# Moving 32x32 turns behind masks on VectorE, and divides ahead of squares on GpSimd, in a fused threshold attention and squared-ReLU MLP

## The chip, the cores and the metric

One core of one Trainium2 chip runs the whole kernel. The metric is the device time of one execution in microseconds; lower is better. All times quoted are medians.

In the profile lines PE is TensorE, PEld its loading of weights, DVE is VectorE, ACT is ScalarE, POOL is GpSimd, and SPq is the queue in which SyncE issues DMAs. L303 is line 303 of the kernel, and `out<-in` names the tiles that an instruction writes and reads. A DMA "lands" when its data are in place.

## The reference

```python
# q, k, v: (8 batches, 8 heads, 576, 64) fp32
scores = q @ k^T / 8                       # (576, 576) per head
thresh = max(scores, -1) - 0.02
scores = where(scores >= thresh, scores, -1e9) - max
attn   = exp(scores) / (sum(exp(scores)) + 1e-9)
x      = (attn @ v) -> (4608, 512)         # heads side by side
out    = relu(x @ w_in)**2 @ w_out         # 512 -> 2048 -> 512
```

## The kernel before

A visit is one pair of heads (the four pairs of the first batch take two short visits each, so 32 pairs make 36 visits). A whole visit has five steps: i = 0 to 3 are 128 queries of both heads each, i = 4 is the last 64 queries of both heads. The MLP works on chunks of 256 tokens, whose matmuls are dealt out between the steps so that TensorE always has something to do. The second product of the MLP is made from seven smaller ones (in all chunks but the first), whose inputs are sums and differences of blocks (the "sums" below). From the twelfth visit on (25 of 36 visits) the weights are turned by VectorE in 32x32 blocks and put into place by DMAs.

Scores are written to PSUM, in which this kernel has room for the scores of one step only. The scores of step s therefore wait until the mask of step s-1 has read them:

```python
def threshold(vis, i):     # VectorE: the mask, L230, and its sums
    for u in range(n):
        nc.vector.scalar_tensor_tensor(out=wu, in0=sc[u], scalar=thr[u], in1=wu,
                                       op0=ALU.is_ge, op1=ALU.mult, accum_out=sm[u])
    nc.vector.tensor_scalar(...); nc.vector.reciprocal(rcp, den)     # L232, L233
def divide(vis, i):        # GpSimd: L240, L242
    nc.gpsimd.tensor_scalar(out=w[:, u, :], in0=w[:, u, :], scalar1=z, scalar2=rcp, op0=add, op1=mult)
```

The turn goes into `turned`, which has two areas; the five steps of a visit fill three (steps 0 and 1, steps 2 and 3, step 4), so a turn can find its area still being read by DMAs. The DMAs put the blocks into `wT`, from which the mix (weights times v) reads. I call the three batches of 16 DMAs P0, P1 and P2:

```python
def turn_blocks(vis, i):   # VectorE, L303
    nc.vector.transpose(wb[:, at:at + k1 - k0, i % 2, :], w[...])
def place_blocks(vis, pair):                       # 16 issues on SyncE's queue
    for qb in range(4):
        for j in range(4):
            nc.sync.dma_start(out=wT[...], in_=wb[...])   # L316: P0, P1; L323: P2
```

The step loop, cut to what matters; `fill(quarter)` emits a quarter of the step's MLP work, with its ReLU (ScalarE), squares and sums (GpSimd, VectorE):

```python
for s in range(END + 1):
    scores(s)                              # TensorE; maximum on VectorE, L207
    # in the 25 late visits at_once is false (but for the first two steps of the first)
    if at_once: exponents(n, i)            # ScalarE: L215, L216, exp L218
    if s in mixes: mix(*mixes[s])          # in step i == 3: the visit before; reads wT
    if 0 < s <= NST and by_dma(steps[s - 1][0]):
        m, x = steps[s - 1]
        turn_blocks(m, x)                  # the step before
        if x >= 2: place_blocks(m, x - 2)  # x = 2: P0, x = 3: P1, x = 4: P2
    fill(quarter)
    if not at_once: exponents(n, i)
    threshold(n, i)
    if last and more: prep(n + 1)          # q and k transposes of the next visit, L181
    fill(quarter)
    divide(n, i)
    fill(quarter); fill(quarter)
```

P1 is thus issued in step 4, right after the turn of step 3.

## Time and profile before

| what | value | how to read it |
|---|---|---|
| time | 1439.11 us, 1432.95 to 1439.48 | median of the first three runs |
| profiled span, clock | 1436.5 us, 0.991 | the traced execution |
| a matmul 128x256 | 383 ns long, the next starts 216 ns later | they overlap, so PE 96% busy is not PE 96% used |
| VectorE's turns (L303) | 325, 168.8 us busy, 31.2 us of waits for DMAs | the waits stand in front of whatever comes behind them |
| issues of P0, P1, P2 | 1200, 0.61 us each and 0.04 to the next | SyncE, one after the other |
| after the last mix | 161.7 us of MLP alone | the same in every kernel of this study |

The prediction shows the lines on which this rests.

### The profile page before, as it was taken

Reading aid. Unit: us, or ns where it says so; the run is one execution under the profiler, and the core shown is the slowest. Engines: PE = TensorE matmul, PEld = TensorE weight load, DVE = VectorE, ACT = ScalarE, POOL = GpSimd, SP = SyncE. Lnnn points to the kernel's source line nnn. Section 1 sums busy time; section 2 is a strip of 40 time slices with the busy share of each in tenths; the row PEclk is TensorE's granted clock in tenths of the full one; section 3 lists DMA queues with packets and bytes.
Section 4 is the critical chain, followed back from the end, with each engine's and each line's share of the span. In section 5 each row is a group of like instructions: output and inputs, shape, how many; then the busy total and the mean of one; then the engine's idle time right before and its main releaser. Section 6 shows DMA issues by size and latency. Waiting matters only on the chain.

```text
span 1436.5 us, 22320 instructions
## 1 busy us (share of the span) xinstructions
PE 1381.1 (96%) x7460; PEld 1066.3 (74%) x7460; DVE 855.2 (60%) x1847; ACT 440.0 (31%) x1080; POOL 772.3 (54%) x1015
## 2 busy tenths in 40 slices
PE   5898989999999999999999999999999999999998
PEld 3676656777777778777777787777777877778887
DVE  5998886875656665656566666565656666401011
ACT  3765655323232223232222232222222222210100
POOL 2687787745554555555464665554546564422332
PEclk9998999999999999999999999999999999999999
DMA  7664441454454545554545455554454556310000
GB/s 150 130 140 111 127 114 41 79 99 89 85 104 84 107 86 113 98 112 82 96 90 101 88 107 91 111 96 92 82 96 89 107 91 112 69 26 9 7 15 15
DMA packets 507201, 127.14 MB, mean 89 GB/s; under 512 B 497488, under 2 KB 499088, under 8 KB 507088
## 3 DMA queue, kind: packets, MB, share of 16 engines
q1 hardware_dynamic: 496208, 107.78, 40.7%
q0 software_dynamic: 8496, 17.64, 4.0%
q8 instruction: 60, 0.98, 0.3%
q10 hardware_dynamic: 2384, 0.30, 0.1%
q14 instruction: 53, 0.43, 0.1%
HBM read 49.81 MB, written 9.44 MB: 41 GB/s over the span
## 4 chain that ended last, share of the span: by engine, by line
PE 59%; SPq 6%; issue 1%; DMA 1%; DVE 1%; POOL 1%; POOLq 0%; DVEq 0%
PE bank L402 24%; PE bank L468 21%; PE s L202 7%; PE bank L359 7%; SPq L316 5%; DMA wT<-turned 1%; SPq L323 1%; DVE turned L303 0%; DVE w L230 0%; POOL vs L176 0%; POOL g L413 0%; DVE gsum L486 0%; POOL vs L173 0%; DVE kT L181 0%; POOL gsum L392 0%
## 5 line engine op out<-in xcount | busy, mean ns | idle before, releaser
L402 PE MATMUL bank<-xT,w_in_sb 128*128 128x256 f32 x2304 | 522.2, 383 | 1.8 <-ACT osb L443 1.8
L402 PEld LDWEIGHTS bank<-xT,w_in_sb 128*128 128x128 f32 x2304 | 433.7, 191 | 82.1 <-issue 21.7
L207 DVE TENSOR_REDUCE st<-s 128x1 f32<-128x576 f32 x288 | 206.9, 753 | 248.2 <-PE s L202 247.8
L230 DVE SCALAR_TENSOR_TENSOR w<-s,st,w 128x576 f32<-128x576 f32 x269 | 207.4, 804 | 97.1 <-ACT w L218 96.9
L242 POOL TENSOR_SCALAR w<-w,st 128x576 f32<-128x576 f32 x269 | 237.9, 892 | 24.8 <-DVE st L233 15.2
L468 PE MATMUL bank<-wo,gsum 128*128 128x256 f32 x1088 | 249.4, 382 | 1.8 <-POOL gsum L392 1.8
L413 POOL TENSOR_TENSOR g<-g 128x512 f32<-128x512 f32 x144 | 150.1, 1045 | 156.2 <-ACT g L412 127.7
L468 PEld LDWEIGHTS bank<-wo,gsum 128*128 128x128 f32 x1088 | 204.4, 190 | 39.9 <-issue 9.8
L202 PE MATMUL s<-kT,qT 64*128 64x288 f32 x1024 | 185.7, 443 | 39.0 <-DVE w L230 19.1
L303 DVE STREAM_TRANSPOSE turned<-w 128x576 f32<-128x576 f32 (+2 forms) x325 | 168.8, 565 | 44.2 <-DMA wT<-turned 31.2
L468 PE MATMUL bank<-wo,g 128*128 128x256 f32 x816 | 188.5, 381 | 0.0
L218 ACT ACTIVATE w<-s,st 128x576 f32<-128x576 f32 x269 | 184.6, 732 | 0.4 <-ACT st L216 0.2
L202 PEld LDWEIGHTS s<-kT,qT 64*128 64x128 f32 x1024 | 105.3, 192 | 102.8 <-issue 75.0
L359 PE MATMUL bank<-wT,vs 128*64 128x128 f32 (+7 forms) x1700 | 172.5, 361 | 5.9 <-DMA wT<-turned 3.1
L468 PEld LDWEIGHTS bank<-wo,g 128*128 128x128 f32 x816 | 153.5, 190 | 28.2 <-issue 7.4
L215 ACT ACTIVATE st<-st 128x2 f32<-128x2 f32 (+1 forms) x160 | 33.4, 209 | 418.8 <-DVE st L207 418.3
L359 PEld LDWEIGHTS bank<-wT,vs 128*64 128x64 f32 (+1 forms) x1700 | 99.7, 138 | 80.2 <-issue 32.3
L240 POOL TENSOR_SCALAR st<-st 128x2 f32<-128x2 f32 (+1 forms) x160 | 39.9, 249 | 207.6 <-DVE w L230 195.0
L412 ACT ACTIVATE g<-bank 128x512 f32<-128x512 f32 x144 | 86.1, 599 | 206.5 <-PE bank L402 206.4
L482 DVE TENSOR_TENSOR gsum<-g 128x512 f32<-128x512 f32 x34 | 21.8, 676 | 110.9 <-PE bank L468 110.9
L346 ACT COPY xT<-bank 128x256 f32<-128x256 f32 x42 | 16.1, 385 | 188.5 <-PE bank L359 188.5
L185 POOL COPY qmid<-qT 64x64 f32<-64x64 f32 x64 | 18.7, 292 | 91.5 <-DVE qT L181 89.7
(68 smaller groups left out, 1009.8 us busy)
## 6 DMA issues: line engine op xcount, KB each, us to landing
wT<-turned SPq DMA_DIRECT2D x800, 72.0 KB, 2.2
ql<-in_q_dram SPq DMA_DIRECT2D x126, 72.0 KB, 2.6
out_dram<-osb POOLq DMA_DIRECT2D x34, 256.0 KB, 2.8
wo<-in_moe_w_in_dram SPq DMA_DIRECT2D x16, 512.0 KB, 4.7
wo<-in_moe_w_out_dram SPq DMA_DIRECT2D x16, 512.0 KB, 3.8
vs<-in_v_dram POOLq DMA_DIRECT2D x50, 128.0 KB, 3.5
kl<-in_k_dram SPq DMA_DIRECT2D x63, 72.0 KB, 2.4
kl<-in_k_dram SPq DMA_DIRECT2D x63, 64.0 KB, 2.5
```

What stands on the lines that cost most here:

```text
L202: nc.tensor.matmul(sc[u][:, half, 0:HALF], lhsT, kT[rows, half * HALF:(half + 1) * HALF], start=True, stop=True)
L207: nc.vector.tensor_reduce(out=mx[:, u:u + 1], in_=sc[u][:, :, 0:HALF], axis=AX.XY, op=ALU.max)
L218: nc.scalar.activation(out=w[:, u, :].rearrange("p (h k) -> p h k", h=2), in_=sc[u][:, :, 0:HALF], func=AF.Exp, bias=bias[:, u:u + 1], sca ...
L230: nc.vector.scalar_tensor_tensor(out=wu, in0=sc[u][:, :, 0:HALF], scalar=thr[:, u:u + 1], in1=wu, op0=ALU.is_ge, op1=ALU.mult, accum_out=s ...
L242: nc.gpsimd.tensor_scalar(out=w[:, u, :], in0=w[:, u, :], scalar1=z[:, u:u + 1], scalar2=rcp[:, u:u + 1], op0=ALU.add, op1=ALU.mult)
L303: nc.vector.transpose(wb[:, at:at + k1 - k0, i % 2, :], w[:, u, k0 * 32:k1 * 32].rearrange("p (k q) -> p k q", q=32))
L316: nc.sync.dma_start(out=to[:, :, at:at + 64], in_=wb[rows, j::4, :, :].rearrange("p c u q -> p c (u q)"))
L359: nc.tensor.matmul(ps[u * D:(u + 1) * D, :], vs[n % 2][rows, u * (NBLK + 1) + c, :], wT[rows, NBLK if c == NBLK else u * (NBLK + 1) + c, a ...
L402: nc.tensor.matmul(h[:, x % 2, :], w_in_sb[:, c, f * P:(f + 1) * P], xT[:, c, at:at + TCH], start=(c == 0), stop=(c == NMC - 1))
L412: nc.scalar.activation(out=to, in_=h, func=AF.Relu)
L413: nc.gpsimd.tensor_tensor(out=to, in0=to, in1=to, op=ALU.mult)
L468: nc.tensor.matmul(to, left[:, f, :], wo[:, slot, f, :], start=(f == 0), stop=(f == HF - 1))
```

## The change

The intent: the mask is what releases PSUM for the next scores, so nothing that isn't needed for it should stand before it. The turns go behind the mask, the exponents before the first quarter of MLP work, and the divide directly behind the mask instead of behind a quarter of squares.

```diff
         if on:
-            if at_once:
-                exponents(n, i)
+            exponents(n, i)
 ...
-        if 0 < s <= NST and by_dma(steps[s - 1][0]):
-            m, x = steps[s - 1]
-            turn_blocks(m, x)
-            if x >= 2:
-                place_blocks(m, x - 2)
         quarter = rate(s) / 4 if s < END else 1e9
         fill(quarter)
 ...
         if on:
-            if not at_once:
-                exponents(n, i)
             threshold(n, i)
             if last and more and not lay:
                 prep(n + 1)
 ...
+            if not at_once:
+                divide(n, i)
+        if 0 < s <= NST and by_dma(steps[s - 1][0]):
+            m, x = steps[s - 1]
+            turn_blocks(m, x)
+            if x >= 2:
+                place_blocks(m, x - 2)
         fill(quarter)
-        if on:
+        if on and at_once:
             divide(n, i)
```

## The prediction

> **What bounds the kernel now.** I read the page first, then the waits of PE and of the DMA queue of SyncE, then the timeline of single steps. A "visit" is one pair of heads: five steps i = 0 to 4, each with scores, maximum, exp, mask and divide; in 25 visits (those that this change touches) VectorE then turns each step's weights in 32x32 blocks into `turned`, and DMAs place the blocks into `wT`, in three batches of 16: P0 (steps 0 and 1), P1 (steps 2 and 3), P2 (step 4). The mix (weights times v) runs in step 3 of the following visit.
>
> The busy shares and the chain of the page:
>
> ```profile
> PE 1381.1 (96%) x7460; PEld 1066.3 (74%) x7460; DVE 855.2 (60%) x1847; ACT 440.0 (31%) x1080; POOL 772.3 (54%) x1015
> ...
> PE 59%; SPq 6%; issue 1%; DMA 1%; DVE 1%; POOL 1%; POOLq 0%; DVEq 0%
> PE bank L402 24%; PE bank L468 21%; PE s L202 7%; PE bank L359 7%; SPq L316 5%; DMA wT<-turned 1%; SPq L323 1%; DVE turned L303 0%; DVE w L230 0%; POOL vs L176 0%; POOL g L413 0%; DVE gsum L486 0%; POOL vs L173 0%; DVE kT L181 0%; POOL gsum L392 0%
> ```
>
> TensorE looks full, and VectorE and GpSimd half idle. But the chain also goes through SPq L316, a queue that only issues DMAs. The waits of that queue say what holds it:
>
> ```profile
> SPq L316 <- PE bank L359: 54.9, 24, 6.9
> SPq L316 <- DVE turned L303: 25.1, 2, 19.1
> ```
>
> 24 times, once a visit, it waits for the mix (L359) to have read `wT`; only twice for a transpose. Its timeline over one visit:
>
> ```profile
> 744.34 21.07 SPq L316 DMA_DIRECT2D wT<-turned  x32
> 765.50 11.01 SPq L323 DMA_DIRECT2D wT<-turned  x16
> 776.55 1.67 SPq L162 DMA_DIRECT2D kl<-in_k_dram  x3
> ```
>
> The mix of the visit before ended at 744.31. The 48 issues then run back to back to 776.51, the last lands at 777.77, and the next mix starts at 780.22. So the queue needs 33.5 us of the 35.9 us between the mixes: a slack of 2.45 us. Over the visits the slack runs from about 0 (417.0, 538.5) to 3.7 us and is mostly 1 to 2. The last mix of all has none: it starts at 1264.57, stops after two matmuls, and resumes at 1268.42 when P2 has landed (1268.22). **The kernel has two bounds of nearly the same length**, TensorE's program order and this loop: mix, 48 issues, landing, mix.
>
> **What TensorE itself still loses.** I took start-to-start distances: a 128x256 matmul follows the one before after 216 ns, eight score matmuls take 1.17 us. What exceeds that by over 0.15 us at a place adds up to 29.8 us between the 24 mixes of the phase 301 to 1229 us, 1.3 us a visit. A typical one:
>
> ```profile
> 406.32 1.44 DVE L303 STREAM_TRANSPOSE turned<-w 128x576 f32<-128x576 f32 x2 [1.60 <-DMA wT<-turned]
> ...
> 407.69 0.77 DVE L230 SCALAR_TENSOR_TENSOR w<-s,st,w 128x576 f32<-128x576 f32 x1
> ...
> 408.62 1.94 PE L202 MATMUL s<-kT,qT 64*128 64x288 f32 x8
> ```
>
> The turn waits 1.60 us for a DMA to free `turned`, the mask behind it is late, and the scores, which need the PSUM that the mask reads, take 1.94 us. This is what the change aims at.
>
> **What the Trainium skill says.** "PSUM — Partial Sum Buffer", section "Engine vs sequencer instructions": the queues of ScalarE, VectorE and GpSimd are strict FIFO. The mask above, stuck behind a turn, agrees, and it is what makes the order matter. "DMA: Bandwidth & Descriptors", section "Anatomy of one DMA": DMA engines do not wait on semaphores, the issuing sequencer waits before dispatch, and a DMA has a fixed cost of about 2 us. The trace agrees: the 16 issues of P1 stand in the queue until their transposes are done (254.04 us, below), and issue to landing is 2.2 us in the median. "GPSIMD Engine Reference", section "8. Key points": GpSimd shares its SBUF interfaces with VectorE, with contention when VectorE reads two SBUF inputs. It agrees: a pair of divisions takes 1.62 us, but 2.68 us at 600.68 beside the subtraction of two SBUF tiles on VectorE (600.74).
>
> **The change, part by part.** It adds and removes no arithmetic; instruction counts and TensorE's order are the same. All of it concerns the 25 late visits.
>
> 1. Exponents go ahead of the first quarter of MLP work. Where ScalarE stood behind the copies of the mix (exp 5.5 us after the maximum at 617 us), it saves the mask that time. Those steps last 11 us, so the mask wasn't late for the scores; worth about nothing by itself.
> 2. The turn goes behind the mask. The turns that wait for `turned` no longer hold up the mask: the list of waits has 31.2 us in 19 waits, most of which vanish. Upper value: the 29.8 us of stalls above.
> 3. The divide goes ahead of the squares: 269 divisions of 892 ns and their small ones start earlier, the squares (1045 ns) up to 2.0 us later. GpSimd is 54% busy. A square is late only where the sums for product 5 are due; I take 0 to 3 us in all.
> 4. **What it moves the wrong way: the turn of step 3.** Its place is step 4, on VectorE. Order now: maximum, turn of 3, mask, q and k transposes (L181) for the next visit. New order: maximum, mask, L181 twice, turn of 3. P1 can't be issued before that turn ends. One visit as it is:
>
> ```profile
> 752.42 0.76 DVE L207 TENSOR_REDUCE st<-s 128x1 f32<-128x576 f32 x1 [2.55 <-PE s L202]
> 753.10 1.55 DVE L303 STREAM_TRANSPOSE turned<-w 128x512 f32<-128x512 f32 x4
> 754.57 0.38 DVE L488 TENSOR_TENSOR osb<-bank,p1s 128x256 f32<-128x256 f32 x1
> 754.88 0.80 DVE L230 SCALAR_TENSOR_TENSOR w<-s,st,w 128x576 f32<-128x576 f32 x1
> ...
> 756.09 0.78 DVE L181 STREAM_TRANSPOSE qT<-ql 128x576 f32<-128x576 f32 x1
> 756.79 0.74 DVE L181 STREAM_TRANSPOSE kT<-kl 128x576 f32<-128x576 f32 x1
> ```
>
> The turn ends at 754.65, P0's sixteenth issue at 754.81: P1 finds its data ready by 0.16 us. In the new order exp of step 4 (about 1.1 us after the maximum) must come first, then mask, its two small operations, L181 twice, and only then 1.55 us of turn. From the mask's start to the end of L181 is 2.65 us; the mask itself can start about 0.3 us earlier. So the turn ends about 3.75 us later: 2.65 - 0.3 + 1.55 - 0.15 of overlap of neighbours on VectorE.
>
> **Sum for the loop.** The turn of 3 ends at one of two distances from the mix, by whether 24 or 32 matmuls of 216 ns lie between mix and scores of step 4: 8.6 us in 14 visits, 10.33 us in 8, 9.7 us in one. From P1's first issue to P2's landing takes 22.1 to 24.1 us, mean 23.15. New distance mix end to next mix start:
> - 14 visits: 8.6 + 3.75 + 0.1 + 23.15 = 35.6 us. Now they have 35.65 us in the mean, 34.2 to 34.3 without their stalls. Visit by visit about zero in all: stalls go, the wait for P2 takes their place.
> - 8 visits: 10.33 + 3.75 + 0.1 + 23.15 = 37.3 us against 35.8 now: +1.5 us each, +12 us.
> - The one at 9.7: +0.4 us.
> - First visit: P1 already waits for the turn (P0 issued by 265.10, turn ends 271.06, P1 starts 271.22), which shows the dependence in this trace. +3.75 less 1.4 of slack: about +2.4 us.
> - Last visit: no q and k to transpose. The turn ends some 2.3 us later, of which P0's end (1245.87 against 1244.45) hides 1.4: +0.9 us.
>
> Together 12 + 0.4 + 2.4 + 0.9 = +15.7 us. After the last mix TensorE runs MLP work alone, unchanged. 1439.1 + 15.7 = 1454.8.
>
> **Rivals.**
> - *The author's*: the mask is the late one, and the kernel gains TensorE's stalls. For it: 1.3 us a visit is really lost. Against: it needs P1 not to wait. If SyncE waited for something else, about 30 us at most would go; more likely 20, giving 1419.
> - *Transfer hidden anyway*: if the turn of 3 is later by under 2 us in the class of 8.6 (P0's issues end 10.5 to 11.5 us after the mix), those visits gain and the other eight lose a little: about 1436.
> - *GpSimd or VectorE becomes the bound*: VectorE's round is now maximum 1.42, exp 1.3 uncovered, mask and small ones 2.0, turn 1.43: 6.1 us in series, where the turn used to lie beside exp; the shortest steps are 6.5 us. With a 1.3 us subtraction between, single steps would slip, and late squares add up to 3 us. If this delays step 3 to step 4 it lies on the loop: up to 1465.
>
> **Range and chances.** The middle is 1455. Downward: a shift of 3.0 instead of 3.75 us takes about 10 us off, and one of the three runs before was 6 us under the median: 1444. Upward: extra slips between mix and the scores of step 4, each in full on the loop: 1464. Slower by 2% would be 1468, faster by 2% 1410, more than all the stalls: both unlikely.
>
> **What would show it.** Right: SyncE's L316 waits for DVE turned L303 in nearly every visit (2 before), some 2 us each; PE L359 waits for DMA wT<-turned, or starts right at the landing; eight visits stretch to about 42 us from mix to mix; DVE turned waiting for DMA (31.2 us) nearly gone; score groups of 1.87 to 1.94 us rarer. Wrong: if P1 starts right behind P0, or the turn of 3 ends under 2 us later than now, or if the time falls under 1432, the stalls were what counted. Mean matmul rows and clock (0.99) should be the same.

## The result, and the profile after

The changed kernel took 1457.14 us (four runs, 1455.09 to 1459.06) against 1439.11: 1.25% longer by the medians. The ratio is 1.0135, with a 95% interval from 1.0104 to 1.0167. A ratio here is the mean time of one kernel's fast runs over that of the other's of the same rounds, so it isn't quite the ratio of the medians. By the 2% rule the two are "same"; by the interval the change is a small loss. The predicted 1455 was 2 us off. That it came so close is partly luck: between the two traces the parts add up to 20.7 us, 5 more than the 15.7 predicted, while the medians lie only 18.0 us apart.

Busy time and the chain on the page of the changed kernel:

```profile
PE 1387.3 (95%) x7460; PEld 1071.6 (74%) x7460; DVE 880.6 (60%) x1847; ACT 440.0 (30%) x1080; POOL 762.7 (52%) x1015
...
PE 72%; SPq 11%; DVE 9%; issue 3%; DMA 2%; ACT 2%; POOL 0%; DVEq 0%; ACTq 0%; POOLq 0%
PE bank L402 27%; PE bank L468 21%; PE s L202 11%; PE bank L359 10%; SPq L323 7%; SPq L316 4%; DMA wT<-turned 2%; DVE w L230 2%; DVE st L207 2%; DVE turned L138 1%; PE bank L266 1%; PE bank L436 1%; DVE wo L426 1%; ACT w L218 1%; DVE turned L137 1%
```

The busy shares hardly differ, and would not tell that 20 us have been added. The chain does: SyncE's queue has gone from 6 to 11%. The waits (engine, line, released by, total us, times, longest) tell more:

```profile
SPq L316 <- DVE turned L303: 81.5, 26, 22.1
SPq L316 <- PE bank L359: 23.0, 21, 6.3
```

Before, the queue waited for a turn twice; now it does 26 times. And on VectorE and TensorE:

```profile
DVE turned L303 <- DMA wT<-turned: 17.1, 45, 1.8
...
PE bank L359 <- DMA wT<-turned: 14.1, 10, 3.9
```

The turns' waits for landings shrank from 31.2 to 17.1 us, as the change intended, and TensorE's waits for landings grew to 14.1 us in 10 times (3.1 us once before). The same visit as in the prediction, on VectorE (start, length, line, tiles, and in brackets the idle time before):

```profile
763.98 0.76 DVE L207 TENSOR_REDUCE st<-s 128x1 f32<-128x576 f32 x1 [2.27 <-PE s L202]
...
765.83 0.82 DVE L230 SCALAR_TENSOR_TENSOR w<-s,st,w 128x576 f32<-128x576 f32 x1 [0.76 <-ACT w L218]
...
767.76 0.74 DVE L181 STREAM_TRANSPOSE kT<-kl 128x576 f32<-128x576 f32 x1
768.42 1.52 DVE L303 STREAM_TRANSPOSE turned<-w 128x512 f32<-128x512 f32 x4
```

The maximum starts 8.1 us after the end of the mix (755.86), as before. The turn now ends 14.1 us after the mix instead of 10.3. On SyncE and TensorE:

```profile
756.15 24.48 SPq L316 DMA_DIRECT2D wT<-turned  x32
780.73 10.99 SPq L323 DMA_DIRECT2D wT<-turned  x16
```

```profile
791.59 0.75 PE L359 MATMUL bank<-wT,vs 128*64 128x320 f32 x2
793.39 4.75 PE L359 MATMUL bank<-wT,vs 128*64 128x320 f32 x38 [1.04 <-issue]
```

The 32 issues of P0 and P1 take 24.5 us instead of 21.1, since the queue stands still from 766.62 to 770.00. P2's last DMA lands at 792.98. The mix starts two of its 40 matmuls, stops, and resumes at 793.39. (The profile names no releaser for this stop, "issue"; that it is the landing is read from the 0.41 us between the two. For ten others the profile names it: the 14.1 us above.)

To say where the 20.7 us between the two traces (1436.5 and 1457.2) came from, I cut both at the ends of the mixes:

| stretch | before | after | difference | predicted |
|---|---|---|---|---|
| start to the end of the first of these mixes | 301.3 | 309.0 | +7.7 | +2.4 |
| from there to the end of the 24th | 932.9 | 944.3 | +11.4 | +12.4 |
| 24th to the last | 40.74 | 42.30 | +1.6 | +0.9 |
| after the last | 161.7 | 161.7 | 0 | 0 |

Inside the 23 mixes of the second row, stops lengthen 16 mixes by 23.8 us in all (2 mixes by 0.7 us before). So the loop added more than 11.4 us; about half of that was paid back by the waits at the scores, which fell from about 16 to about 4 us from 301 us on (what the switches to scores and back exceed their usual length by, see turn3_first).

### The profile page after: what moved, and what is told of

It reads as the page before. It is cut to its first block, busy times and chain, and to the rows that moved or that the text cites. A ratio compares the mean times of both kernels' runs of the same rounds, so it can differ in the third digit from the quotient of the medians.

```text
span 1457.2 us, 22482 instructions
## 1 busy us (share of the span) xinstructions
PE 1387.3 (95%) x7460; PEld 1071.6 (74%) x7460; DVE 880.6 (60%) x1847; ACT 440.0 (30%) x1080; POOL 762.7 (52%) x1015
## 4 chain that ended last, share of the span: by engine, by line
PE 72%; SPq 11%; DVE 9%; issue 3%; DMA 2%; ACT 2%; POOL 0%; DVEq 0%; ACTq 0%; POOLq 0%
PE bank L402 27%; PE bank L468 21%; PE s L202 11%; PE bank L359 10%; SPq L323 7%; SPq L316 4%; DMA wT<-turned 2%; DVE w L230 2%; DVE st L207 2%; DVE turned L138 1%; PE bank L266 1%; PE bank L436 1%; DVE wo L426 1%; ACT w L218 1%; DVE turned L137 1%
## 5 line engine op out<-in xcount | busy, mean ns | idle before, releaser
L402 PEld LDWEIGHTS bank<-xT,w_in_sb 128*128 128x128 f32 x2304 | 433.6, 191 | 82.4 <-issue 21.1
L242 POOL TENSOR_SCALAR w<-w,st 128x576 f32<-128x576 f32 x269 | 225.0, 844 | 24.9 <-DVE st L233 16.3
L202 PE MATMUL s<-kT,qT 64*128 64x288 f32 x1024 | 180.5, 442 | 39.7 <-DVE w L230 16.7
L359 PE MATMUL bank<-wT,vs 128*64 128x128 f32 (+7 forms) x1700 | 184.8, 362 | 19.9 <-DMA wT<-turned 14.1
L359 PEld LDWEIGHTS bank<-wT,vs 128*64 128x64 f32 (+1 forms) x1700 | 110.0, 139 | 96.1 <-issue 54.3
L303 DVE STREAM_TRANSPOSE turned<-w 128x576 f32<-128x576 f32 (+2 forms) x325 | 167.6, 563 | 18.8 <-DMA wT<-turned 17.1
L202 PEld LDWEIGHTS s<-kT,qT 64*128 64x128 f32 x1024 | 101.2, 191 | 101.8 <-issue 72.7
L143 POOL TENSOR_TENSOR turned<-turned 128x512 f32<-128x512 f32 x32 | 41.2, 1287 | 44.6 <-DVE turned L141 42.3
```

Source lines behind the costliest of these rows:

```text
L202: nc.tensor.matmul(sc[u][:, half, 0:HALF], lhsT, kT[rows, half * HALF:(half + 1) * HALF], start=True, stop=True)
L303: nc.vector.transpose(wb[:, at:at + k1 - k0, i % 2, :], w[:, u, k0 * 32:k1 * 32].rearrange("p (k q) -> p k q", q=32))
L359: nc.tensor.matmul(ps[u * D:(u + 1) * D, :], vs[n % 2][rows, u * (NBLK + 1) + c, :], wT[rows, NBLK if c == NBLK else u * (NBLK + 1) + c, a ...
L402: nc.tensor.matmul(h[:, x % 2, :], w_in_sb[:, c, f * P:(f + 1) * P], xT[:, c, at:at + TCH], start=(c == 0), stop=(c == NMC - 1))
```

## The experiments

Eleven kernels ran in three groups, each beside the kernel before on the same chip (1438.44, 1435.93 and 1436.61 us). Kernels of different groups are compared by medians, and the kernel before moved by some 3 us between the groups. The theory is that the late turn of step 3 holds P1 in the queue, and the loop of mix, 48 issues and landing becomes the bound. The rivals were that the early divides delay the squares, or that turns behind masks lengthen VectorE's round in general. The cuts by mixes of each kernel (first mix's end, to the 24th, to the last; us; without p2_from_act, which is set aside below) come first:

```
before                 301.3   932.9   40.7
after                  309.0   944.3   42.3
turn3_first            307.6   926.8   41.9
turn3_behind_alone     308.1   974.1   42.6
turn3_between          306.9   940.9   42.4
divide_late            308.6   945.6   41.5
turns_first            301.4   935.3   40.4
turn0_behind_alone     301.1   926.4   39.5
turn3_first_v0_old     301.4   926.2   40.4
turns_0_3_behind       303.4   944.5   41.6
half_p2                306.8   919.4   36.1
turn0_mask4_ahead      301.7   920.2   40.4
```

### turn3_first: one turn back

```diff
+        if 0 < s <= NST and by_dma(steps[s - 1][0]) and steps[s - 1][1] == 3:
+            ...turn_blocks, place_blocks         # ahead of fill and mask
         quarter = rate(s) / 4 if s < END else 1e9
...
-        if 0 < s <= NST and by_dma(steps[s - 1][0]):
+        if 0 < s <= NST and by_dma(steps[s - 1][0]) and steps[s - 1][1] != 3:
```

> The changed kernel, with only the turn of step 3 (and the issue of P1 behind it) put back ahead of the mask of step 4; the turns of the other four steps stay behind the masks, exponents and divide stay early. My theory (P1 held back by that turn, the loop mix - 48 issues - landing - mix is the bound): P1 again starts right behind P0, the loop needs 33.4 to 35.0 us between mixes, TensorE's own order without stalls 33.4 to 35.3, the larger of the two summed over 23 visits is 797 us against 822 in the kernel before: about 1415 to 1424 us, faster than both kernels. Rival 1 (the early divides that delay the squares cost the time) or rival 2 (any turn behind the mask lengthens VectorE's round): 1445 us or more.

Measured: 1437.26 us, ratio 0.9986 (0.9944 to 1.0028). Moving this one turn back took 20 us off the changed kernel, and P1 again starts 0.12 us behind P0 in the mean (2.11 in the changed kernel). The direction is the theory's. But the kernel isn't faster than before, and my 1415 to 1424 was a clear miss. Two causes show in the trace. First, the steady part is 6.1 us shorter than before, not 25: my figure for TensorE's stalls was too large. A switch from the MLP's matmuls to the eight score matmuls of steps 0 to 2 and back costs 0.20 us in both kernels when nothing waits: the first score starts 0.31 us after the matmul before it, and after the scores the second MLP matmul starts 0.32 us after the first, both instead of 0.216. Of the 29.8 us in the prediction about 14 are this fixed cost at 69 switches, and only about 16 us were waits. Second, the first visit still loses 6.3 us here (307.6 against 301.3), so that isn't P1's doing alone. (1.6 us more went where the granted clock fell to half for a moment, see the next run.)

### turn3_behind_alone: only the suspected part

In the kernel before, only the turn of step 3 moves behind the mask and the q and k transposes.

```diff
-        if 0 < s <= NST and by_dma(steps[s - 1][0]):
+        if 0 < s <= NST and by_dma(steps[s - 1][0]) and steps[s - 1][1] != 3:
...                                               # behind threshold and prep, ahead of fill:
+        if 0 < s <= NST and by_dma(steps[s - 1][0]) and steps[s - 1][1] == 3:
```

> The kernel before, with only the turn of step 3 moved behind the mask of step 4 and the q and k transposes; exponents, divide and the other turns as before. My theory: the full loss of the loop, about 1450 to 1457 us, with SyncE's L316 waiting for the transpose L303 in over 20 visits. Rivals 1 and 2 (divide early, or the other four turns): within 5 us of before, 1434 to 1444.

Measured: 1486.72 us, ratio 1.034 (1.0306 to 1.0375), worse than the whole change by 30 us. P1 is held back as foreseen (2.13 us behind P0), but most of the time is lost elsewhere, and the size is a miss. The waits of this kernel:

```profile
DVE turned L303 <- DMA wT<-turned: 67.9, 20, 4.9
PE s L202 <- DVE w L230: 46.1, 33, 3.5
```

One case in its timeline, on VectorE and then on TensorE:

```profile
799.26 1.44 DVE L303 STREAM_TRANSPOSE turned<-w 128x576 f32<-128x576 f32 x2 [3.20 <-issue]
800.62 0.78 DVE L230 SCALAR_TENSOR_TENSOR w<-s,st,w 128x576 f32<-128x576 f32 x1
```

```profile
801.56 1.94 PE L202 MATMUL s<-kT,qT 64*128 64x288 f32 x8 [1.57 <-DVE w L230]
```

P1, now late, frees its area of `turned` late. The turn of step 0 of the next visit needs that area, and here it still stands ahead of the mask. The mask waits with it, and the scores wait for the mask. (The profile gives the turn's idle time to "issue"; P1's last DMA landed at 798.89.) There is next to no stop inside the mixes: TensorE lost the time earlier, at the scores, where the waits rose from about 16 to about 48 us.

That is 32 of the 41 us by which the steady part grew. The other 10 or so are the clock: in six stretches of 4 to 10 matmuls the MLP's matmuls follow each other after 0.43 us instead of 0.216, and the clock granted to TensorE is 0.50 there (759 to 763 us, for instance). Each stretch begins within 4 us after a gap of 1.5 to 3.6 us between the starts of two matmuls. Gaps of 2.2 us in the kernel before (at 450.5 and 1043.5) were followed by none, so the runs don't show which gap brings it on.

So a late P1 can be paid for in two places, and the change had closed this one by its other moves.

### turn3_between: half the dose

```diff
             threshold(n, i)
+            if 0 < s <= NST and by_dma(steps[s - 1][0]) and steps[s - 1][1] == 3:
+                ...turn_blocks, place_blocks
             if last and more and not lay:
                 prep(n + 1)
...                                               # and the turn of step 3 leaves its later place
```

> The changed kernel, with the turn of step 3 between the mask of step 4 and the q and k transposes (L181). A dose: the turn ends some 1.5 us earlier than in the changed kernel, 2.25 us later than before. My theory: the loop is then 34.1 us (14 visits) and 35.8 us (8 visits), close to TensorE's own 33.4 to 35.3: about 1424 to 1434 us. Rival 1: no difference to the changed kernel, 1457.

Measured: 1451.69 us, ratio 1.0101 (1.0068 to 1.0134): better than the changed kernel by 5 us, and a miss of 18 us. The turn did end 1.3 us earlier (11.0 and 12.8 us after the mix). What I had left out is that the k transpose, now behind the turn, releases the next visit's first scores:

```profile
PE s L202 <- DVE kT L181: 31.1, 16, 8.5
```

In the changed kernel this wait has 15.4 us in 3 times. The stops inside the mixes fell from 23.8 to 3.1 us, but most of this gain at P1 went to a new wait at the scores of step 0.

### divide_late: the divide back behind the squares

```diff
-            if not at_once:
-                divide(n, i)
...
-        if on and at_once:
+        if on:
             divide(n, i)
```

> The changed kernel, with the divide back behind the second quarter's squares as before. My theory: the loop from visit to visit is unchanged (about 41.0 us a visit); only the first visit may give back the 3 to 5 us that its subtractions (L426: 0.69 us each before, 1.16 us after) lost beside GpSimd's two-input adds: 1452 to 1457 us. Rival 1 (late squares are the cost): back to 1436 to 1442.

Measured: 1458.79 us, ratio 1.0149 (1.012 to 1.0179), the same as the changed kernel, and 1.8 us above my range. The early divide neither costs nor gains anything that these runs resolve, and rival 1 has fallen. The first visit's loss didn't come back either (308.6), so the early divide isn't its cause, as I had thought possible.

### turns_first: exponents and divide alone

```diff
         # the changed kernel; the whole block turn_blocks / place_blocks back ahead of
         quarter = rate(s) / 4 if s < END else 1e9
```

> The changed kernel with all five turns back ahead of the masks: only the early exponents and the early divide are left of the change. My theory: these two are worth nearly nothing, 1433 to 1441 us, VectorE again waiting about 30 us for landings ahead of the turn of step 0. Rival (early divides cost by delaying the squares): 1445 or more.

Measured: 1436.85 us, ratio 1.0009 (0.9988 to 1.003). Early exponents and early divides together are worth nothing. The order of the turns is the whole change.

### turn0_behind_alone: only the turn that waits

As turn3_behind_alone, with `== 0` and `!= 0`.

> The kernel before, with only the turn of step 0 moved behind the mask of step 1 (it is the one that waits for P1's landing, the 31.2 us of DVE turned waiting for DMA); all else as before. Theory: the late masks and thereby late scores go, 17.1 us of PE waits beyond the fixed 0.2 us at each switch shrink to some 5, P1 and P2 keep their times; mixes then meet the landing now and then: 1424 to 1432 us. Rival (the waits don't matter, the landing sets the end anyway): 1435 to 1440.

Measured: 1427.19 us, ratio 0.9943 (0.9924 to 0.9961), faster than both kernels by a little. The waits of the turns for DMAs fall from 31.2 to 4.0 us, and the waits at the scores beyond the fixed cost from about 16 to about 6 us over the phase from 301 us on. This is what was good in the change.

### turns_0_3_behind: the square closed

As turn3_behind_alone, with `in (0, 3)` and `not in (0, 3)`.

> The kernel before with the turns of steps 0 and 3 behind the masks, the rest as before; with before (1436 to 1439), turn 0 alone (1427) and turn 3 alone (1487) this closes a square of four. If the 48 us of turn 3 alone are 18 of late P1 at the mix plus 30 of masks held up by the turn of step 0 that waits for the late P1, then putting turn 0 behind its mask removes the second part: 1452 to 1460 us. If the parts simply add: 1475 to 1480.

Measured: 1451.62 us, ratio 1.0105 (1.0081 to 1.0129), 0.4 us under my range. The four corners are 1436 to 1439 (neither), 1427 (turn 0), 1487 (turn 3) and 1452 (both). If the parts added, both would give about 1476. Putting turn 0 behind its mask removes the path through the mask, and the 25.0 us of stops inside 16 mixes appear in its place, as in the changed kernel (23.8 us in 16). My split of the 48 us into 18 at the mix and 30 at the masks was wrong in one point: with turn 3 alone nothing is lost at the mix, since TensorE, delayed before it, finds P2 landed. It is at the masks, and some 10 us of it at the halved clock, of which this kernel has nothing in the steady part.

### p2_from_act: another queue, inconclusive

```diff
-                    nc.sync.dma_start(out=to[:, c:c + n, at:at + 32], in_=wb[rows, first::4, 0, :])
+                    # kept, then two after each fill(quarter) of the next steps:
+                    nc.scalar.dma_start(out=to, in_=src)
```

> The changed kernel, order of VectorE unchanged (turn of step 3 as late as there), but the 16 issues of P2 go to ScalarE's queue, two after each quarter of the next visit's steps 1 and 2. The loop on SyncE shrinks by 10 us, so P1's late start should no longer reach the mix. My theory (late turn costs only through the queue): the waits inside the mix (25.3 us in 24 mixes of the changed kernel, 7 in the last) go, SyncE still waits for the transpose in every visit: 1425 to 1436 us. If the late turns cost through VectorE's round instead: 1450 or more.

Measured: 1711.86 us, ratio 1.1928 (1.1907 to 1.195). The experiment did not do what it was made for. Its waits:

```profile
SPq L324 <- DMA wT<-turned: 229.7, 61, 10.1
```

SyncE's own issues of P0 and P1 (L324 there) now wait for DMAs that write `wT`; before, such waits were not among the queue's. Presumably the program has to order two queues that write one tile, which one queue needed no wait for; I haven't isolated it. It says nothing about the theory.

### half_p2: the loop made shorter

The same question, asked without a second queue. Half of P2 is left out, so the result is wrong (relative error 0.29); the order on all engines is that of the changed kernel.

```diff
+                    if qb % 2:
+                        continue
                     first = j if qb < 2 else (j - KB) % 4
```

> The changed kernel with 8 of P2's 16 issues left out (wrong result on purpose: 32 of 64 columns of wT stay old); order on every engine otherwise as in the changed kernel, so the turn of step 3 is as late as there. The queue needs 5 us less between turn and mix. My theory (the late turn costs only through the 32 issues behind it): the 25 us of waits inside the 24 mixes go, some 5 of 7 us of the last one too: 1425 to 1434 us, with SyncE still waiting for the transpose. Rival (the late turns cost on VectorE or through GpSimd): 1450 or more.

Measured: 1425.85 us, ratio 0.993 (0.9905 to 0.9955), 31 us under the changed kernel. SyncE's queue and the mix:

```profile
SPq L316 <- DVE turned L303: 99.8, 33, 22.1
```

```profile
775.89 4.79 PE L361 MATMUL bank<-wT,vs 128*64 128x320 f32 x40
```

The queue still waits for the late turn, more than ever. But no mix of the 23 stops (4.79 us each), and the steady part falls from 944.3 to 919.4 us. So from the first mix on, the late turn costs nothing on VectorE or GpSimd that would show; it costs through the issues that stand behind it. Two limits: leaving out issues shortens the loop whatever the turn does, so the 31 us are not all the late turn's (the last stretch, 36.1 us, falls below that of the kernel before); and the first visit still loses 5.5 us here (306.8). That it is the turn of step 3 that makes the loop too long is what turns_0_3_behind shows beside turn0_behind_alone, from which it differs in this turn alone: stops of 25.0 us in 16 mixes against 2.3 us in 4.

### turn3_first_v0_old: the first visit

turn3_first, with the turns of the first of the 25 visits where they were (`s <= first_dma + 5`).

> turn3_first, with the order of before for the turns of the first of the 25 visits. Theory: turn3_first lost about 6 us there, because its six subtractions (L426) ran beside two-input adds of GpSimd (1.16 us each instead of 0.69) and the maximum of step 4 stood behind them; with the old order they run beside the divides again. Expected 1428 to 1434 us; if the first visit isn't the reason, 1436 to 1440 as turn3_first.

Measured: 1428.12 us, ratio 0.9942 (0.9925 to 0.996). The first visit ends at 301.4 us again. There VectorE also makes sums of the output weights (L426, subtractions of two SBUF tiles), six in a row. In the kernel before, VectorE and GpSimd ran:

```profile
264.79 4.15 DVE L426 TENSOR_TENSOR wo<-wo 128x512 f32<-128x512 f32 x6
```

```profile
265.04 4.42 POOL L242 TENSOR_SCALAR w<-w,st 128x576 f32<-128x576 f32 x2 [0.26 <-DVE st L233]
```

and in the changed kernel:

```profile
267.53 6.97 DVE L426 TENSOR_TENSOR wo<-wo 128x512 f32<-128x512 f32 x6
```

```profile
269.49 1.59 POOL L392 TENSOR_TENSOR gsum<-g 128x512 f32<-128x512 f32 x1
271.16 1.59 POOL L393 TENSOR_TENSOR gsum<-gsum,g 128x512 f32<-128x512 f32 x1
```

With a turn ahead of them, the six start 2.7 us later, miss the divides and meet GpSimd's two-input sums instead: 6.97 us rather than 4.15. The maximum of step 4 stands behind them, and TensorE waits 6.59 us for the k transpose at 279.07 (1.91 us at 273.76 before). That the old order cures it is shown. How it comes about is read from the traces and not isolated: the maximum of step 4 starts 5.6 us later (2.7 from the later start of the six, 2.8 from their length), and from the maximum to the end of the turn of step 3 it takes 3.7 us more, so that P1 starts at 280.52 instead of 271.22. The same traces show both bounds again. In turn3_first P1 starts at 277.17 and P2 lands 2.1 us before the mix, but the visit still loses 6.3 us, so there it is not the queue that holds it but the scores behind the k transpose (they wait 6.83 us); in turns_0_3_behind, where the six are not slowed, P1 starts 3.8 us later and the visit loses 2.1.

### turn0_mask4_ahead: a better kernel

turn0_behind_alone, and in step 4 alone exponents, mask and q and k transposes go ahead of the first quarter's sums:

```diff
+        if on and ahead:                # ahead = by_dma(n) and i == NBLK and not at_once
+            threshold(n, i)
+            if more: prep(n + 1)
         quarter = rate(s) / 4 if s < END else 1e9
```

> turn0_behind_alone, and in step 4 the exponents, the mask and the q and k transposes ahead of the first quarter's sums on VectorE (the turn of step 3 stays first). In turn0_behind_alone 6 switches to the scores still lose 6.9 us, where the transposes of k stood behind mask and sums. If that is their cause: 1419 to 1424 us; if not, 1425 to 1430.

Measured: 1424.53 us, ratio 0.9915 (0.9897 to 0.9933): the fastest correct kernel by its median, though its interval overlaps that of turn0_behind_alone, and half a microsecond outside what I expected. The waits at the switches to the scores beyond the fixed cost fell from about 6 to 2.6 us in all.

## Why the prediction was right or wrong

- **Two bounds of nearly the same length.** Right. half_p2 shows the loop from one side (with a shorter queue and the same late turn no mix stops, and the steady part is 25 us shorter than in the changed kernel), turns_0_3_behind from the other (beside turn0_behind_alone, the turn of step 3 alone brings stops of 25.0 us in 16 mixes, against 2.3 us in 4).
- **Turn of step 3 later by 3.75 us.** Right from the second visit on: it ends 12.3 and 14.1 us after the mix, predicted 12.35 and 14.1.
- **Sum for the loop.** +11.4 us in the steady part against +12.4 predicted. The eight visits did reach 41.7 to 42.75 us from mix end to mix end. They add 11.7 us by themselves, and the other 15 take 0.3 off, which is the prediction visit by visit. In these eight, P1 had 0.15 to 1.4 us to spare in the kernel before (from the end of the turn to the end of P0's issues), in the other 15 it had 1.7 to 2.9.
- **The turn of step 0 no longer holds up the mask.** Right, and turn0_behind_alone gives its value alone, about 9 us. Waits of 31.2 us fell to 17.1, not to nearly nothing: they are now short waits, 45 of them, behind the mask.
- **"What TensorE itself still loses", 29.8 us.** This term was mis-sized. About 14 us of it are the fixed 0.2 us at 69 switches to scores, so about 16 us were to be had. The prediction survived it, because the loop and not this term set the new time in most visits. It failed at once where it was asked alone, in turn3_first.
- **First visit, +2.4 us.** Mis-sized: +7.7. The step that failed is the shift of the turn, for which I took the 3.75 us of the later visits; here P1 starts 9.3 us later. From the maximum of step 4 on, the shift is 3.7 us as predicted, but the maximum itself is 5.6 us late: the moved turn of step 2 pushes six subtractions of VectorE beside two-input work of GpSimd, and the maximum stands behind them.
- **Last visit, +0.9 us.** +1.6.
- **Early divide, 0 to 3 us; early exponents, about nothing.** Right: divide_late and turns_first show no difference.
- **Rival of VectorE's round.** In the changed kernel not seen as a wait at the scores. But my own expectations for turn3_behind_alone and turn3_between fell for lack of it: each time a wait removed or moved in step 4 came back one step later.

What stays open: why SyncE's issues waited for other DMAs once ScalarE issued a part of them, and what the slower subtractions of the first visit cost by themselves.

## What to carry to other kernels

Before moving an instruction behind another on a FIFO engine, look up who waits for it, and not only who waits for what it blocked. Here one of five equal-looking turns had 32 DMA issues behind it, in eight visits with 0.15 to 1.4 us to spare, and another stood in front of the mask for nothing. Moving only the second gained 0.6%, where moving all five, with exponents and divide, lost 1.35%. A queue that only issues DMAs can be a bound of its own: add up its issues and compare with the distance between what starts and what ends them.

## What the Trainium skill lacked or had wrong

- "DMA: Bandwidth & Descriptors", section "Issuing engines are not separate DMA queues", says that the time a sequencer takes to initiate a DMA is usually small relative to the DMA itself. Here one issue of a small strided DMA on SyncE takes 0.61 us plus 0.04 to the next, 48 of them 31 to 33 us of every 40, against 2.2 us from issue to landing. No page that I read says for how long an issue from SyncE holds its queue.
- "GPSIMD Engine Reference", section "8. Key points", says that GpSimd and VectorE contend when VectorE reads two SBUF inputs, and gives no size in that place. Here five of six subtractions of two SBUF tiles on VectorE stay at 0.67 to 0.69 us beside divides of GpSimd with one tile input (one takes 1.15), and a divide goes from 0.81 to 2.2 us. Beside GpSimd's two-input work the six subtractions take 6.97 us instead of 4.15, with single ones up to 1.75 us, and GpSimd's sums 1.59 instead of 1.27 us.
- "TensorEngine Tiling (Array Packing)", section "Key Properties", says that changing the tiling mode drains TensorE, without a figure. Here a switch from MLP matmuls (128*128 in the profile) to scores of 64 rows (64*128) and back costs 0.20 us at 69 switches, and a switch to the 128-row scores of step 4 (128*128) and back costs nothing at 24: the next matmul starts after the usual 0.216 us. The cost goes with the shape; that the drain is its reason is not isolated.
